# A recurrent-attention and gated-mixing kernel on one core: Wk loaded in quarters, one K group, one wait and one sum moved

## The chip, the cores and the metric

The kernel runs on one core of a Trainium2 chip. The core has a matrix engine (TensorE, in the rows PE, its weight loads PEld), a vector engine (VectorE, DVE), an activation engine (ScalarE, ACT), a general engine (GpSimd, POOL) and an engine that issues the DMAs (SyncE, SP). They run at their own pace and wait for each other through semaphores; each engine takes its instructions in the order of the program. TensorE multiplies a stationary operand, brought in by a weight load, with a moving operand that streams past, and writes its result to PSUM, which has eight banks. The metric is the time of one execution in device microseconds; of several runs the median counts.

## The reference

Two blocks are computed one after the other over a sequence of 2048 rows of 512 values, in bf16. Block A is attention with a recurrent memory: the sequence is cut into 64 segments of 32 rows, and 8 memory rows stand in front of each. What a segment's memory rows become is the memory of the next segment, so the 64 segments can't be computed side by side.

```
mem = mem0
for s in range(64):
    h = concatenate([mem, x_normed[32 * s : 32 * s + 32]])      # 40 rows
    q, k, v = h @ Wq, h @ Wk, h @ Wv                            # 32 heads of 128
    p = softmax(where(mask, q @ k.T * scale, -1e9))             # memory rows visible to all, the rest causal
    o = (p @ v) @ Wo
    mem, out[s] = o[:8], o[8:]
h = x + out
z = gelu(layernorm(h) @ w_in)                                   # block B, 512 -> 1792
z1, z2 = z[:, :896], layernorm(z[:, 896:])
h2 = h + (z1 * (w_sp @ z2 + b_sp)) @ w_out                      # w_sp mixes the 2048 rows
```

## The kernel before

All instructions are written out by a Python program that adds operations to the five engines' queues in one order (`em.add`, with the tokens each operation reads and writes); from the tokens it works out which waits each operation needs, and leaves out those that an earlier wait of the same engine covers already.

**Start.** x blocks and the weights are loaded by SP, in one queue. The last 8 of each segment's 32 x rows are treated apart: their Q, K and V are computed for 16 segments at once, ahead of the steps, as wide matmuls, in groups of 16 (four heads by four contraction chunks of 128, function `qkx_mm`, line 432). At the start 28 such groups run for the first chunks of segments: sixteen with Wq, then twelve with Wk (`start_x`). They rotate over four PSUM banks (`ebank`), and their evacuation alternates between ACT and DVE (`qkx_evac`, lines 441 and 443). Between them DVE computes the layer-norms of three x blocks (`ln_stats`, `ln_apply`, lines 379 to 389), with two small POOL operations in each. Then come the first wide V groups (line 457).

**The 64 steps.** A step has 32 stationary columns (8 memory rows, 24 x rows) in a slot of `hT`, in four contraction chunks `dc`. Chunk by chunk they are loaded as weights into the four column tiles of TensorE, 32 columns each, and four matmuls, one a tile, stream four different parts of the projection's weights past them. Four such matmuls of 512 columns are a "group" below. Where two groups in a row use the same chunk, the second can do without its weight loads: it is "held" (`tile_mm(..., held=True)`, recorded at line 515; with loads, line 514). A step is, in the order of TensorE:

- `QK(s, 0, 0)` and `QK(s, 0, 1)`: Q and K of the first 16 heads, chunk 0 first; then `mem_out(s - 1, 1)` (line 716), which transposes half of the former step's memory rows by matmuls with a selecting matrix; ACT copies them into `hT` (line 721), chunks 2 and 3. Then the other chunks.
- `QK(s, 1, 0)`: Q of the second 16 heads; `K1(s, 0, ...)` and `K1(s, 1, ...)`: K of the second 16 heads in two banks (3 and 7) of 256 columns, in the chunk order 3, 0, 1, 2 and 3, 0, 2, 1. ACT copies each out of PSUM (lines 551, 541), DVE transposes it (lines 563, 548).
- `S_half` (lines 585 and 591): scores of a half of the heads, with a mask that DVE puts into the bank ahead (line 575); exponential on ACT (line 599), sums over the keys on TensorE (line 606 and a held part), logarithm and reciprocal on ACT, normalisation on POOL and DVE (line 625, 631). Between them stand the groups of `V_half`.
- `PV_half` (lines 659 and 665): probabilities by V; line 665 uses the V of the 8 other rows (`Vx`, brought in by a DMA that step s - 1 issues). Then `Wo` (again line 514, with `cT`), `part_evac` and `mem_out(s, 0)`.
- In gaps, further work: wide groups for later segments, `WoX_mm` (line 743) for the 8 other rows, `F_group` (line 728), which sums four segments' results into a block of 128 rows, and from step 44 on the first matmuls of block B (`z2_narrow`, line 811).

Bank 7 serves, one after the other, the last K quarter-bank, PV and the second half of `Wo` (`OB2`), which DVE copies out (`part_evac`, line 709); `mem_out(s, 1)` reads that copy.

**Instruction blocks.** A planner (`plan`, `weight_of`, `block_cost`) counts TensorE's instructions from the program's first one, takes it that they are fetched in blocks of 256, and wants no block to begin at certain places of a step. It does so by `spare`: that many of a step's held groups are given their weight loads after all, which lengthens the step by four instructions each. `WAITS` and `STEP` stand for wait instructions of TensorE that the program can't count while it is written: so many before the loop, so many in each step. Looking four steps ahead, it takes the cheapest k from 0 to 8:

```
FETCH, FETCH0, WAITS, STEP = 256, 191, 11, 2
...
    return 4 if 338 <= place < 378 else 1 if 318 <= place < 338 or 148 <= place < 196 else 0
...
    n = 588 + 24 * (s % 4 == 2) + 8 * (s >= 3 * CK)
...
spare[0] = plan(s, pe_count[0] + WAITS + STEP * s)[1] if s else 0
```

**Behind the steps.** Block B's z2 for the last row blocks: row block 13 (`direct`) is computed straight from `z2_mm` in its narrow form (line 811), then the last `F_group(RB - 1, XB)`, the last `WoX_mm`, and the wide matmuls of z1, of the mixing (line 1352) and of the output (line 1476). `XB` is bank 3; the addition before this F (`h_done`, `F_add`, line 733, on DVE) reads it.

## Time and profile before

| | us |
|---|---|
| median of 3 runs | 843.62 (843.14 to 846.21) |
| the profiled execution | 844.33 |
| its span, first to last instruction | 842.6 |
| TensorE (PE) busy | 831.7, 99% |
| weight loads (PEld) busy | 435.8, 52% |
| VectorE (DVE) busy | 525.5, 62% |
| ScalarE (ACT) busy | 469.4, 56% |
| GpSimd (POOL) busy | 128.0, 15% |
| granted clock of TensorE | 0.999 |

The profile is of one execution; its times count from the span's start. A row of a timeline gives the start, the time, the engine, the line, the operation, what it writes and reads, and how many instructions are merged; in brackets stands the idle time before and what ended it. "128*32 128x512" is a matmul with 128 rows and 32 columns of weights and 512 columns of moving data. The end of a matmul is modelled, and four of a group run side by side, so starts are to be compared with starts. A row of the waits gives total time, number and longest wait. "Issue" is a wait that no semaphore explains.

### The profile page before, as it was taken

The numbers are of one execution on the slowest core, as the hardware profiler recorded it, in microseconds if no ns is written. First come the engines' busy times: TensorE is split into PE (matmuls) and PEld (weight loads), VectorE is DVE, ScalarE is ACT, GpSimd is POOL, SyncE is SP. The second block draws the span as 40 slices with busy tenths as digits, with TensorE's granted clock in tenths as the row PEclk, the third lists the DMA queues.
The fourth block names the chain that finished last, engine by engine and source line by source line (L and its number), as shares of the span: only waits on it lengthen the run. The fifth ranks groups of instructions, "written<-read, shape, count | busy, mean of one in ns | idle before, by whom it ended". The sixth has DMA issues, their size and how long they took to land.

```text
span 842.6 us, 45239 instructions
## 1 busy us (share of the span) xinstructions
PE 831.7 (99%) x22069; PEld 435.8 (52%) x19133; DVE 525.5 (62%) x1321; ACT 469.4 (56%) x1250; POOL 128.0 (15%) x340
## 2 busy tenths in 40 slices
PE   9999999999999999999999999999999999999998
PEld 9754555455555554545554555554555554444443
DVE  3556667676666666676666666766666666654443
ACT  3456665667676766667666666666666666500000
POOL 5011111111111111111111121111111113300000
PEclk9999999999999999999999999999999999999999
DMA  9962222322222232121223233233333479033001
GB/s 319 395 203 54 72 66 60 79 54 61 60 57 48 54 48 66 43 68 48 73 50 88 54 77 75 77 83 84 83 77 74 91 244 340 1 113 111 28 14 39
DMA packets 111877, 78.62 MB, mean 93 GB/s; under 512 B 65976, under 2 KB 103872, under 8 KB 111680
## 3 DMA queue, kind: packets, MB, share of 16 engines
q1 hardware_dynamic: 111680, 75.67, 32.2%
q8 instruction: 163, 2.67, 1.4%
q14 instruction: 34, 0.28, 0.1%
HBM read 43.16 MB, written 22.12 MB: 77 GB/s over the span
## 4 chain that ended last, share of the span: by engine, by line
PE 95%; DMA 2%; SPq 1%; DVE 1%; ACT 0%; issue 0%; POOL 0%
PE f_ps L514 45%; PE f_ps L515 12%; PE f_ps L1352 11%; PE f_ps L743 4%; PE f_ps L1476 3%; PE f_ps L659 3%; PE f_ps L1345 2%; PE f_ps L811 2%; PE f_ps L451 2%; PE f_ps L432 2%; DMA f_arena<-in_A_Wk_dram 2%; PE f_ps L585 1%; PE f_ps L606 1%; PE f_ps L457 1%; PE f_ps L716 1%; PE f_ps L665 1%
## 5 line engine op out<-in xcount | busy, mean ns | idle before, releaser
L514 PE MATMUL f_ps<-f_arena,f_hT 128*32 128x512 bf16 (+1 forms) x4996 | 358.3, 356 | 0.5 <-issue 0.3
L514 PEld LDWEIGHTS f_ps<-f_arena,f_hT 128*32 128x32 bf16 x4996 | 123.6, 96 | 152.4 <-issue 57.2
L515 PE MATMUL f_ps<-f_arena,f_hT 128*32 128x512 bf16 (+1 forms) x2172 | 173.4, 333 | 0.0
L551 ACT ACTIVATE f_Tst<-f_ps 128x512 bf16<-128x512 f32 x224 | 127.1, 597 | 60.7 <-PE f_ps L514 60.7
L514 PE MATMUL f_ps<-f_arena,f_cT 128*32 128x256 bf16 x3844 | 128.7, 272 | 1.2 <-ACT f_cT L678 0.5
L514 PEld LDWEIGHTS f_ps<-f_arena,f_cT 128*32 128x32 bf16 x3844 | 94.1, 96 | 29.4 <-ACT f_cT L678 19.6
L1352 PE MATMUL f_ps<-f_arena 128*128 128x512 bf16 x448 | 101.0, 379 | 0.6 <-DVE f_arena L1338 0.4
L563 DVE STREAM_TRANSPOSE f_QT<-f_Tst 128x256 uint32<-128x256 uint32 x128 | 57.1, 446 | 67.2 <-ACT f_Tst L551 67.2
L651 DVE CAST f_V_sb<-f_ps 128x512 bf16<-128x512 f32 (+1 forms) x128 | 71.0, 555 | 42.2 <-PE f_ps L514 42.2
L680 DVE TENSOR_SCALAR f_cT<-f_ps 128x320 bf16<-128x320 f32 x128 | 56.9, 487 | 28.5 <-PE f_ps L665 28.5
L1352 PEld LDWEIGHTS f_ps<-f_arena 128*128 128x128 bf16 x448 | 43.5, 98 | 54.0 <-DVE f_arena L1338 2.0
L709 DVE CAST f_part<-f_ps 128x256 bf16<-128x256 f32 x64 | 27.2, 425 | 63.5 <-PE f_ps L514 63.5
L599 ACT ACTIVATE f_E_sb<-f_ps 128x224 bf16<-128x224 f32 x128 | 46.2, 361 | 36.7 <-PE f_ps L591 36.7
L570 POOL COPY f_QT<-f_arena 128x128 uint32<-128x128 uint32 x64 | 18.8, 294 | 300.3 <-PE f_ps L591 300.1
L678 ACT ACTIVATE f_cT<-f_ps 128x320 bf16<-128x320 f32 x128 | 49.0, 435 | 23.0 <-PE f_ps L665 22.9
L721 ACT ACTIVATE f_hT<-f_ps 128x16 bf16<-128x16 f32 x126 | 23.3, 185 | 54.4 <-PE f_ps L716 54.0
L1358 DVE TENSOR_TENSOR f_arena<-f_ps,f_arena 128x512 f32<-128x512 f32 x28 | 19.3, 690 | 51.4 <-PE f_ps L1352 48.7
L575 DVE CAST f_ps<-f_mask 128x224 f32<-128x224 bf16 x128 | 47.0, 368 | 0.0
L621 ACT ACTIVATE f_R_sb<-f_R_sb 128x160 f32<-128x160 f32 x128 | 43.2, 338 | 4.0
L541 ACT ACTIVATE f_Tst<-f_ps 128x256 bf16<-128x256 f32 x128 | 42.2, 381 | 3.7
L700 POOL COPY f_cTx<-f_cT 128x256 bf16<-128x256 bf16 x64 | 25.4, 397 | 121.7 <-DVE f_cT L680 121.7
L707 ACT ACTIVATE f_part<-f_ps 128x256 bf16<-128x256 f32 x64 | 24.6, 385 | 31.8 <-PE f_ps L514 31.8
(130 smaller groups left out, 1216.1 us busy)
## 6 DMA issues: line engine op xcount, KB each, us to landing
wT_d<-f_wst SPq DMA_DIRECT2D x64, 128.0 KB, 3.1
f_arena<-wT_d SPq DMA_DIRECT2D x32, 256.0 KB, 4.7
f_arena<-in_A_Wk_dram SPq DMA_DIRECT2D x2, 2048.0 KB, 13.8
f_arena<-in_A_Wv_dram SPq DMA_DIRECT2D x2, 2048.0 KB, 23.3
f_arena<-in_A_Wo_dram SPq DMA_DIRECT2D x8, 512.0 KB, 9.3
f_Vx<-vext_d SPq DMA_DIRECT2D x63, 64.0 KB, 2.7
f_arena<-in_A_Wq_dram SPq DMA_DIRECT2D x3, 1024.0 KB, 10.5
vext_d<-f_Vs SPq DMA_DIRECT2D x24, 128.0 KB, 2.2
```

What stands on the lines that cost most here:

```text
L514: return e.matmul(out, lhsT=lhsT, rhs=rhs, start=start, stop=stop, skip_group_check=True, tile_position=(0, 32 * c))
L515: return e.add_instruction(mybir.InstMatmult(name=nc.get_next_instruction_name(), ins=[e.lower_ap(rhs), e.lower_ap(lhsT)], outs=[e.lower_a ...
L541: act(lambda e: e.activation(out=Tst[:, 1, 256 * k:256 * k + 256].rearrange("p (gi r) -> p gi r", r=2), in_=ps[:, bank, 0:256].rearrange(" ...
L551: act(lambda e: e.activation(out=Tst[:, tb, :].rearrange("p (C gi r) -> p C gi r", C=2, r=2), in_=ps[:, bank, :].rearrange("p (C r gi) -> ...
L563: dve(lambda e: e.transpose(out=dst, in_=Tst[:, mi, :].bitcast(U32)), reads=[("T", mi, 0), ("T", mi, 1)], writes=wr)
L575: dve(lambda e: e.tensor_copy(out=ps[:, bank, 0:224], in_=mask[:, :]), reads=["mask"], writes=[PB(bank)])
L599: act(lambda e: e.activation(out=E_sb[:, b, :], in_=ps[:, bank, 0:224], func=ACT.Exp, scale=scale, bias=SHIFT), reads=[PB(bank)], writes=[ ...
L621: act(lambda e: e.activation(out=R_sb[:, b, :], in_=R_sb[:, b, :], func=ACT.Exp, scale=-1.0, bias=RBIAS), reads=[("R", b)], writes=[("R", b)])
L651: dve(lambda e: e.tensor_copy(out=V_sb[:, b, cs], in_=ps[:, bank, cs]), reads=[PB(bank)], writes=wr)
L678: act(lambda e: e.activation(out=dst, in_=src, func=ACT.Copy, scale=UNSC), reads=[PB(PVB[c])], writes=[("cT", c)])
L680: dve(lambda e: e.tensor_scalar(out=dst, in0=src, scalar1=UNSC, scalar2=None, op0=ALU.mult), reads=[PB(PVB[c])], writes=[("cT", c)])
L1352: pe(lambda e: e.matmul(ps[:, bank, 0:TB], lhsT=z2[:, sc, fb * 128:(fb + 1) * 128], rhs=wTb[tb % 2][:, :, sc, :], start=(n == 0), stop=(n ...
```

## The change

Five edits:

1. Wk is loaded as quarter 0, quarter 1 and the second half, in place of two halves: one DMA more on SP's queue.
2. In steps from 1 on, `K1(s, 1, 0)`, the chunk-0 group of the last K quarter-bank (bank 7), runs directly behind `mem_out(s - 1, 1)`, with weight loads of its own, and opens the accumulation; it was the fourth of the K1 groups and held. `K1(s, 1, 3)` no longer opens it.
3. The last group of `V_half(s, 1)` waits, in its fourth column tile, for the DMA of the Vx rows, which line 665 waited for before.
4. Behind the steps, `F_group(RB - 1, XB)` comes after both z2 matmul sets of the direct row block, in place of between them.
5. The planner counts 592 for 588 instructions a step, 13 for 11 waits before the loop and 1 for 2 in each step.

```diff
-    def V_half(s, b, dcs=range(DC), held=None):
+    def V_half(s, b, dcs=range(DC), held=None, also=()):
...
-                   reads=[("hTx", (s // 4) % 3), ("hTm", s, dc // 2), ("W", 2, 2 * b), ("W", 2, 2 * b + 1)], writes=[PB(bank)])
+                   reads=[("hTx", (s // 4) % 3), ("hTm", s, dc // 2), ("W", 2, 2 * b), ("W", 2, 2 * b + 1), *(also if c == 3 else ())], writes=[PB(bank)])
...
-    for hf in range(2):
-        load_wh(1, hf)
+    load_w(1, 0)
+    load_w(1, 1)
+    load_wh(1, 1)
...
-    FETCH, FETCH0, WAITS, STEP = 256, 191, 11, 2
+    FETCH, FETCH0, WAITS, STEP = 256, 191, 13, 1
...
-        n = 588 + 24 * (s % 4 == 2) + 8 * (s >= 3 * CK)
+        n = 592 + 24 * (s % 4 == 2) + 8 * (s >= 3 * CK)
...
             mem_out(s - 1, 1)
+        if s:
+            K1(s, 1, 0, True, False, False)
         QK(s, 0, 1, (1,), 0, 2)
...
-        K1(s, 1, 3, True, False, bool(hold(True)))
+        K1(s, 1, 3, not s, False, bool(hold(True)))
         K1(s, 0, 0, False, False, False)
-        K1(s, 1, 0, False, False, bool(hold(True)))
+        if not s:
+            K1(s, 1, 0, False, False, bool(hold(True)))
...
-            V_half(s, 1, (2,))
+            V_half(s, 1, (2,), also=[("Vx", s % NVX)])
...
         z2_mm(rb, 0, zbank(), True)
+        z2_mm(rb, 1, zbank(), True)
         if k == 0:
             F_group(RB - 1, XB)
-        z2_mm(rb, 1, zbank(), True)
```

## The prediction

> **What bounds the kernel now.** I read the page first, then the waits of PE and PEld, then the timelines of the start, of two steps and of the seam behind the last step.
>
> ```profile
> span 842.6 us, 45239 instructions
> ...
> PE 831.7 (99%) x22069; PEld 435.8 (52%) x19133; DVE 525.5 (62%) x1321; ACT 469.4 (56%) x1250; POOL 128.0 (15%) x340
> ...
> GB/s 319 395 203 54 72 66 60 79 54 61 60 57 48 54 48 66 43 68 48 73 50 88 54 77 75 77 83 84 83 77 74 91 244 340 1 113 111 28 14 39
> ...
> q8 instruction: 163, 2.67, 1.4%
> ```
>
> ```profile
> PE f_ps L432 <- DMA f_arena<-in_A_Wk_dram: 1.4, 1, 1.4
> ...
> PEld f_ps L514 <- ACT f_hT L721: 33.6, 107, 0.4
> ```
>
> TensorE is the bound: 99% busy, and no other engine passes 62%. PE itself shows only one wait of over a microsecond that the change touches, 1.4 us for Wk. So no part can win much, and the prediction is a sum of small holes. "Busy" hides some of them: the end of a matmul is modelled, so a hole shows as a late start of the next group of four matmuls (one per column tile). I read starts against starts. The holes are of three kinds: the Wk wait; short waits at fixed places of each of the 64 steps; and irregular holes at the edges of instruction blocks (q8: 163 packets, 2.67 MB, so fetches of 16 KB, for 41,202 PE and PEld instructions, about one per 256).
>
> **Part 1, Wk in quarters and a half.** The first Wk group of matmuls needs only the first quarter of Wk.
>
> ```profile
> 21.93 0.41 PE L397 MATMUL f_ps<-f_ident,f_part 128*32 128x128 bf16 x16
> 23.77 2.84 PE L432 MATMUL f_ps<-f_hTe,f_arena 128*128 128x128 bf16 x48 [1.43 <-DMA f_arena<-in_A_Wk_dram]
> ...
> 39.39 1.90 PE L457 MATMUL f_ps<-f_arena,f_hTe 128*128 128x512 bf16 x8
> ...
> 23.74 0.69 DVE L443 CAST f_arena<-f_ps 128x512 bf16<-128x512 f32 x1
> ...
> 9.84 2.54 SPq L318 DMA_DIRECT2D f_arena<-in_A_Wk_dram  x2
> 12.42 7.58 SPq L318 DMA_DIRECT2D f_arena<-in_A_Wv_dram  x2
> ...
> f_arena<-in_A_Wk_dram SPq DMA_DIRECT2D x2, 2048.0 KB, 13.8
> f_arena<-in_A_Wv_dram SPq DMA_DIRECT2D x2, 2048.0 KB, 23.3
> ```
>
> The half issued at 9.84 lands at 23.64. Its second megabyte takes about 2.65 us at the page's 395 GB/s, so the first quarter lands near 21.0 and is there when PE is ready at 22.34 (21.93 + 0.41). The second, near 23.7, is wanted by the third group, later than 24. The 1.43 us wait on the DMA goes. But something else is late next. The groups of this stage rotate over four PSUM banks, and the second Wk group takes the bank of the fourteenth Wq group, whose evacuation is the DVE cast of 23.74. It ends at 24.43, held up behind the layer-norm of three x blocks, which does not depend on Wk. Today that second group starts at 23.77 + 0.9 = 24.67 (a third of the 2.84 us, less its part of the tail of the last matmul). It can't start before 24.49, 0.06 after the cast (the distance from an end on DVE or ACT to the start on PE in the rows of parts 2 and 3). **Gain 0.18 us, not 1.43**; PE will wait some 1.2 us for DVE in place of the DMA. Ends: 0, and 1.43 if that cast were earlier too. SP issues one DMA more, and the Wv loads queue behind it. They are issued from 12.42 on, take 23.3 us, and their first reader starts at 39.39: slack of over 3 us hides an issue of at most 2.5 us. One more wait stands in PE's stream, before the loop, inside the stretch that waits anyway: nothing.
>
> **Part 2, the quarter of the last K moved into the mem rows' shadow.** In each step from 1 on, the second half of mem_out transposes mem rows 2 and 3 by matmul, ACT copies them (L721), and the weights of contraction chunk 2 wait for the copy.
>
> ```profile
> 256.51 0.18 ACT L721 ACTIVATE f_hT<-f_ps 128x16 bf16<-128x16 f32 x1
> ...
> 256.30 0.39 PE L514 MATMUL f_ps<-f_arena,f_hT 128*32 128x512 bf16 x4
> 256.51 0.39 PE L515 MATMUL f_ps<-f_arena,f_hT 128*32 128x512 bf16 x4
> 256.75 0.61 PE L514 MATMUL f_ps<-f_arena,f_hT 128*32 128x512 bf16 x8
> 257.19 0.39 PE L515 MATMUL f_ps<-f_arena,f_hT 128*32 128x512 bf16 x4
> ...
> 257.83 0.82 PE L514 MATMUL f_ps<-f_arena,f_hT 128*32 128x512 bf16 x12
> 258.48 0.39 PE L515 MATMUL f_ps<-f_arena,f_hT 128*32 128x256 bf16 x8
> 258.70 0.28 PE L514 MATMUL f_ps<-f_arena,f_hT 128*32 128x256 bf16 x4
> 258.81 0.28 PE L515 MATMUL f_ps<-f_arena,f_hT 128*32 128x256 bf16 x4
> ...
> 648.36 0.39 PE L515 MATMUL f_ps<-f_arena,f_hT 128*32 128x512 bf16 x4
> ...
> 649.03 0.39 PE L515 MATMUL f_ps<-f_arena,f_hT 128*32 128x512 bf16 x4
> ```
>
> Three groups of 512 columns take 0.65 us undisturbed (257.83 to 258.48). Across the wait they take 0.68 (256.51 to 257.19) in step 21 and 0.67 (648.36 to 649.03) in step 60; over steps 2 to 62 the mean excess is 0.028 us. The copy ends at 256.69, PE goes on at 256.75. A group of 256 columns (0.11 us, 258.70 to 258.81) put before 256.30 moves the reader from 256.73, where two groups of 0.215 would let it start, to 256.84, past the copy: the hole closes. The group itself costs nothing net, being only moved. **Gain 63 x 0.028 = 1.76 us.** Its bank, number 7, was freed by the same part copy that mem_out waits for anyway, so no wait is added.
>
> It needs its own weight loads, four a step, where it used the loaded ones before. A pair of such held groups takes 0.22 (258.48 to 258.70), a loaded one 0.11: no difference, so I take zero, hidden beside the 0.11 us of matmul.
>
> What else the move does: the Q and first K projections end 0.11 us closer to the scores that need them.
>
> ```profile
> 259.34 0.45 DVE L563 STREAM_TRANSPOSE f_QT<-f_Tst 128x256 uint32<-128x256 uint32 x1
> 259.78 0.59 DVE L548 STREAM_TRANSPOSE f_KT<-f_Tst 128x128 uint32<-128x128 uint32 x2
> ...
> 259.36 0.66 ACT L541 ACTIVATE f_Tst<-f_ps 128x256 bf16<-128x256 f32 x2
> ...
> 260.45 0.27 PE L585 MATMUL f_ps<-f_QT,f_KT 128*32 128x40 bf16 x16
> ```
>
> DVE's transposes are a queue: Q's (259.34) shifts by 0.11 and ends at 259.90. The two of the last K start now at 259.78, released by ACT, whose two copies end at about 259.75 and 260.02; the first moves to some 259.83, the second, released at 260.02, needs to move by 0.00 to 0.05. They end at 260.37 now, and the second scores start at 260.45, a slack of 0.03 over the 0.06 from DVE's end to PE. So 0 to 0.02 us a step come back. I take 0; 63 x 0.02 = 1.3 us is the unfavourable end.
>
> **Part 3, the V rows' wait.** The wait for the Vx rows' DMA leaves PV, where it stands as an instruction of its own beside a wait for DVE, for the fourth column tile of a long V group. The DMA is issued a whole step ahead of its reader, so the wait holds up nobody for data.
>
> ```profile
> 262.34 0.33 DVE L625 TENSOR_TENSOR f_E_sb<-f_R_sb,f_E_sb 128x160 bf16<-128x160 f32 x1
> ...
> 262.66 0.21 PE L665 MATMUL f_ps<-f_E_sb,f_Vx 32*128 32x64 bf16 x4
> ...
> 262.73 0.31 PE L659 MATMUL f_ps<-f_E_sb,f_V_sb 32*128 32x40 bf16 x16
> ```
>
> Here the second PV half starts at 262.73, 0.06 after DVE's normalisation ends (262.67), and the Vx matmuls ahead of it have time to spare: an earlier 262.66 is lost there. That is so in 32 steps (12 to 43). In some 30 others PE runs through, and the pause ahead of L665 exceeds its neighbours' by 0.012 us. **Gain 30 x 0.012 = 0.35 us**; ends 0.75 (all steps) and a loss of 0.6 (0.01 in the V group in each).
>
> **Part 4, the F sums behind the second matmul of the direct row block.**
>
> ```profile
> 687.73 0.68 DVE L733 TENSOR_TENSOR f_hbuf<-f_ps,f_hbuf 128x512 bf16<-128x512 f32 x1
> ...
> 687.38 0.93 PE L811 MATMUL f_ps<-f_arena 128*32 128x448 bf16 x16
> 688.47 0.75 PE L728 MATMUL f_ps<-f_part,f_F_sb 128*32 128x512 bf16 x4 [0.16 <-DVE f_hbuf L733]
> ```
>
> Four groups of 448 columns (0.19 each, in proportion to 0.216) end at 688.14; F waits for its bank until DVE's addition ends at 688.41. The next four z2 groups fill 0.76 us of PE, past that end: **gain 0.33 us** (0 if the fetch hole that also falls on this F group, part 5, stays there). F's only reader, the WoX scatter into the same bank, stands well behind in the program, so F is late for nobody; the z2 result and its gelu come earlier.
>
> **Part 5, instruction blocks.** The stream grows by three instructions a step, so all block edges move, and the planner (new constants) spends other "unheld" loads. At some edges PE stands:
>
> ```profile
> 295.10 0.56 PE L514 MATMUL f_ps<-f_arena,f_cT 128*32 128x256 bf16 x8
> ...
> 475.22 0.28 PE L514 MATMUL f_ps<-f_arena,f_cT 128*32 128x256 bf16 x3
> 475.88 0.38 PE L514 MATMUL f_ps<-f_arena,f_cT 128*32 128x256 bf16 x5 [0.39 <-issue]
> ```
>
> Within one group 0.66 us pass from 475.22 to 475.88; the group of 295.10 lasts 0.56 where two quiet ones take 0.39. Between these 256-instruction edges from 295.10 to the last at 688.47 (L728 in the fence before: 0.75 where 0.39 is due) I count 13 such holes of over 0.08 us, 4.2 us together. They mostly follow blocks that begin shortly before PV, with many short instructions, which PE runs through fastest, so that the next fetch is late. Stepping the planner's formula through the steps of before, with 4 - 1 instructions more in each, I get 14 such blocks from step 24 on where there are 13 now. So I take no change, with 1.7 us to either side. The Trainium skill (Runtime: NRT & Kernel Launch, Instruction fetch mechanics) says that fetch goes in 16 KiB blocks of 256 instructions and that crossing one is mostly hidden. The block size agrees with the 2.67 MB in 163 fetches; 13 of some 160 edges not being hidden is what costs here.
>
> **The sum.** 0.18 + 1.76 + 0.35 + 0.33 = 2.6 us. The profiled execution takes 844.33 us (span 842.6, 1.7 around it); it would become 841.7. It stands 0.7 above the median of 843.62, within the runs shown. Against the median: **841.0 us**. A change of 0.5% (4.2 us) is about what a measurement of this kernel can tell; by that mark I forecast no change.
>
> **Rivals.**
> - The DVE queue takes the place of the mem rows (slower). If the full 0.11 us reaches the second K transpose, the second scores wait 0.11 - 0.03 = 0.08 us a step: 5.1 us lost, 1.76 won; with the other parts 843.62 + 2.5 = 846.1. It decides from a delay of 0.07 us on. For it: DVE's rows touch end to end. Against: the two K transposes wait for ACT today, which absorbs most.
> - The four loads a step don't hide (slower).
>
> ```profile
> L514 PEld LDWEIGHTS f_ps<-f_arena,f_cT 128*32 128x32 bf16 x3844 | 94.1, 96 | 29.4 <-ACT f_cT L678 19.6 <-issue 1.2
> ```
>
> A load costs the load path 94.1 / 3844 = 0.0245 us; 252 of them in the open are 6.2 us: 841.0 + 6.2 = 847.2. It decides from 0.010 us a load. Against it speaks the 0.11 of the group with loads at 258.70, as long as the held ones. The Trainium skill (TensorE: Matmul & The Clock Gate, Part 3, The mechanism) says that weight loads overlap matmuls in flight only where the row group differs; the four column tiles of a group here share theirs. By this rule the rival would hold; the rows at 258.48 and 258.70 don't agree with it for column tiles.
>
> - Block edges fall worse or better: 14 blocks at the 0.3 us that a hole costs on average, in place of 13 holes, is no change; all 14 at 0.5 us gives 7.0 for 4.2 us, 843.8, half of the holes gone 838.9. The dice are thrown anew.
> - The start wins the whole 1.43 us: 839.7. It needs DVE's cast at 23.74 to be earlier; its x blocks are loaded ahead of Wk as before, so I see no reason.
> - Part 2 does nothing, a later wait takes it: 842.8.
>
> **How the numbers follow.** The forecast, with block edges within 1 us of before, has 0.55. Block edges worse by more than that (about 843.5, at the worst 845): 0.13; better (839): 0.08. Part 2 does nothing: 0.09. The DVE queue: 0.06. The whole start: 0.06. The weight loads: 0.03. The forecast's own range is 839.4 to 842.6, from the ends of part 3 and 1 us of edges. Eight in ten are reached by taking in the better half of the edges' good side, the lost part 2 and the edges' bad side: **838.8 to 844.6**. Faster by over 0.5% means under 839.4: the better edges mostly, half of the whole start, a rest of the forecast's tail, 0.10. Slower by over 0.5% means over 847.8: a part of the weight loads and of the DVE queue together with bad edges, 0.04. The rest, 0.86, lies within 0.5%.
>
> **What the profile of after would show.** Part 1: no wait of L432 on the Wk DMA, but one of 1.2 us on the DVE cast L443 in the same place; the first Wv group earlier by 0.2 us, not by 1.4. Part 2: behind the mem rows' transposition a 256-column group, and three groups of 512 columns behind it in 0.65 us; the wait of PEld on ACT's L721 shorter by its half; the second scores still 1.09 us behind the first (260.45 against 259.36, where the held group of 258.48 and its followers end); the quiet steps 0.03 us shorter. Part 3: no change in the distance of the second PV half from DVE's L625 in steps 12 to 43. Part 4: L728 starts without a wait. Part 5: about a dozen holes at block edges, 3 to 6 us together, in other steps.
>
> Wrong would make it: a transposition chain on DVE that shifts by more than I read from its overlaps; a wait on bank 7 that I have missed, which would stand in front of the moved group in every step; or a planner whose count is off by a few instructions, so that block edges fall into PV in many steps.

## The result, and the profile after

The changed kernel takes 840.83 us (median of 6 runs, 840.04 to 840.97); beside it the kernel before took 845.41 (6 runs, 843.14 to 846.28). The ratio is 0.9951, with a 95% interval of 0.9936 to 0.9965. Repeated on another chip, it took 840.38 us beside 843.33, ratio 0.9969 (0.9957 to 0.9981). So the kernel is 1.6 to 5.4 us faster; 4.1 and 2.6 us are the middles of the two intervals. The forecast was 841.0 us, 2.6 less than the 843.62 that was known then.

The page of the changed kernel, profiled in an execution of 840.04 us:

```profile
span 838.3 us, 45576 instructions
...
PE 827.7 (99%) x22059; PEld 446.4 (53%) x19541; DVE 518.2 (62%) x1321; ACT 465.7 (56%) x1250; POOL 128.0 (15%) x340
```

TensorE is still the bound. The view of waits, as "engine line <- what it waited for: us in total, times, longest":

```profile
PE f_ps L432 <- DVE f_arena L443: 1.2, 1, 1.2
```

```profile
PEld f_ps L514 <- ACT f_hT L721: 30.7, 111, 0.4
```

The wait for Wk's DMA has become a wait for DVE of nearly the same length, and the weight loads wait for ACT's copies of the mem rows 2.9 us less (33.6 before). The timeline of the start (start, duration, engine and line; the idle time before it in brackets):

```profile
21.92 0.41 PE L397 MATMUL f_ps<-f_ident,f_part 128*32 128x128 bf16 x16
22.26 1.07 PE L432 MATMUL f_ps<-f_hTe,f_arena 128*128 128x128 bf16 x16
24.49 1.96 PE L432 MATMUL f_ps<-f_hTe,f_arena 128*128 128x128 bf16 x32 [1.16 <-DVE f_arena L443]
26.38 0.41 PE L397 MATMUL f_ps<-f_ident,f_part 128*32 128x128 bf16 x16
```

```profile
23.74 0.69 DVE L443 CAST f_arena<-f_ps 128x512 bf16<-128x512 f32 x1
```

The first Wk group runs at 22.26, as soon as PE is free. The second starts at 24.49, 0.06 after DVE's cast ends at 24.43. These last two times stand in the forecast to the hundredth; for the first it had 22.34.

Step 21 has these rows; they are about one microsecond earlier than the same step of before:

```profile
255.33 0.22 PE L716 MATMUL f_ps<-f_G_sb,f_part 128*32 128x8 bf16 x8
255.39 0.50 PE L514 MATMUL f_ps<-f_arena,f_hT 128*32 128x256 bf16 x8
255.72 0.39 PE L515 MATMUL f_ps<-f_arena,f_hT 128*32 128x512 bf16 x4
255.93 0.61 PE L514 MATMUL f_ps<-f_arena,f_hT 128*32 128x512 bf16 x8
256.36 0.39 PE L515 MATMUL f_ps<-f_arena,f_hT 128*32 128x512 bf16 x4
...
258.42 0.27 PE L585 MATMUL f_ps<-f_QT,f_KT 128*32 128x40 bf16 x16
...
259.51 0.27 PE L585 MATMUL f_ps<-f_QT,f_KT 128*32 128x40 bf16 x16
```

Behind the mem rows' transposition stand the moved quarter (four matmuls of the row at 255.39, 0.11 us) and four groups of 512 columns (0.215 each): 0.97 us are due, and 255.39 to 256.36 is 0.97. The hole is closed. ACT's copy and the weight loads that wait for it are there as before:

```profile
255.60 0.18 ACT L721 ACTIVATE f_hT<-f_ps 128x16 bf16<-128x16 f32 x1
```

```profile
255.84 0.20 PEld L514 LDWEIGHTS f_ps<-f_arena,f_hT 128*32 128x32 bf16 x8 [0.34 <-ACT f_hT L721]
```

The loads still start 0.06 us behind the copy, which ends at 255.78, but their matmuls are due only at 255.93. So the wait of the loads stays in the view of waits, and PE no longer sees it. The second scores still stand 1.09 us behind the first. At the seam:

```profile
684.02 0.68 DVE L733 TENSOR_TENSOR f_hbuf<-f_ps,f_hbuf 128x512 bf16<-128x512 f32 x1
```

```profile
683.67 1.69 PE L811 MATMUL f_ps<-f_arena 128*32 128x448 bf16 x32
685.18 0.39 PE L728 MATMUL f_ps<-f_part,f_F_sb 128*32 128x512 bf16 x4
685.39 1.90 PE L743 MATMUL f_ps<-f_arena,f_cTx 128*32 128x512 bf16 x32
```

The eight z2 groups run through, and F finds its bank free for 0.48 us (684.70 to 685.18).

Where the 4.3 us between the two profiled spans came from: the first scores start 0.32 us earlier (41.22 to 40.90); 62 steps, in the median 9.950 us long, became 9.919, 1.9 us; the seam gave 0.35. The rest, some 1.7 us, is the holes at block edges: 12 of over 0.1 us with 4.09 us together before, 8 with 2.36 after. That last item is what most of the experiments went to.

### The profile page after: what moved, and what is told of

The parts are those of the page before. It is cut to its first block, busy times and chain, and to the rows that moved or that the text cites. A ratio compares the mean times of both kernels' runs of the same rounds, so it can differ in the third digit from the quotient of the medians.

```text
span 838.3 us, 45576 instructions
## 1 busy us (share of the span) xinstructions
PE 827.7 (99%) x22059; PEld 446.4 (53%) x19541; DVE 518.2 (62%) x1321; ACT 465.7 (56%) x1250; POOL 128.0 (15%) x340
## 4 chain that ended last, share of the span: by engine, by line
PE 95%; DMA 1%; DVE 1%; ACT 1%; SPq 0%; issue 0%; POOL 0%
PE f_ps L514 47%; PE f_ps L1356 11%; PE f_ps L515 11%; PE f_ps L743 4%; PE f_ps L659 3%; PE f_ps L1480 3%; PE f_ps L1349 2%; PE f_ps L811 2%; PE f_ps L451 2%; PE f_ps L432 2%; DMA f_part<-in_A_x_dram 1%; PE f_ps L585 1%; PE f_ps L606 1%; PE f_ps L716 1%; PE f_ps L457 1%; PE f_ps L665 1%
## 5 line engine op out<-in xcount | busy, mean ns | idle before, releaser
L514 PE MATMUL f_ps<-f_arena,f_hT 128*32 128x512 bf16 (+1 forms) x5404 | 359.3, 351 | 0.3
L514 PEld LDWEIGHTS f_ps<-f_arena,f_hT 128*32 128x32 bf16 x5404 | 135.4, 96 | 138.7 <-issue 50.2
L551 ACT ACTIVATE f_Tst<-f_ps 128x512 bf16<-128x512 f32 x224 | 127.1, 597 | 65.3 <-PE f_ps L514 65.3
L515 PE MATMUL f_ps<-f_arena,f_hT 128*32 128x512 bf16 (+1 forms) x1764 | 146.7, 341 | 0.0
L721 ACT ACTIVATE f_hT<-f_ps 128x16 bf16<-128x16 f32 x126 | 23.2, 184 | 53.9 <-PE f_ps L716 53.4
L541 ACT ACTIVATE f_Tst<-f_ps 128x256 bf16<-128x256 f32 x128 | 42.1, 381 | 0.1
```

Source lines behind the costliest of these rows:

```text
L514: return e.matmul(out, lhsT=lhsT, rhs=rhs, start=start, stop=stop, skip_group_check=True, tile_position=(0, 32 * c))
L515: return e.add_instruction(mybir.InstMatmult(name=nc.get_next_instruction_name(), ins=[e.lower_ap(rhs), e.lower_ap(lhsT)], outs=[e.lower_a ...
L541: act(lambda e: e.activation(out=Tst[:, 1, 256 * k:256 * k + 256].rearrange("p (gi r) -> p gi r", r=2), in_=ps[:, bank, 0:256].rearrange(" ...
L551: act(lambda e: e.activation(out=Tst[:, tb, :].rearrange("p (C gi r) -> p C gi r", C=2, r=2), in_=ps[:, bank, :].rearrange("p (C r gi) -> ...
```

## The experiments

**1. Is it DVE's order that limits part 1?** The layer-norm work of three x blocks is spread over later evacuations, so that the cast the second Wk group waits for comes earlier. The second kernel does the same with Wk in two halves, as before. (Where an edit changes the number of instructions or waits, the planner's constants follow; these lines are left out here and below.)

```diff
-        if 11 <= n < 14:
-            ln_apply(n - 7)
-        if 10 <= n < 13:
-            ln_stats(n - 6)
+        if n in (11, 13, 15):
+            ln_apply(4 + (n - 11) // 2)
+        if n in (10, 11, 13):
+            ln_stats((4, 5, None, 6)[n - 10])
```

> The changed kernel, with DVE's evacuation of the fourteenth Wq group put ahead of the layer-norm work of the second and third x block (the same operations in another order). My theory: the quarters of Wk came in time, and only that cast holds the start. Then the wait of L432 on DVE (1.16 us) goes, the matmuls behind the second x transposition start near 25.3 instead of 26.72, the first scores come 1.3 to 1.4 us earlier, and the median falls from 840.8 to about 839.5. Rival: the second quarter, POOL's layer-norm operations or another bank hold PE next; then the start wins under 0.4 us and the median stays within 0.4 of the changed kernel's.

```diff
-    load_w(1, 0)
-    load_w(1, 1)
-    load_wh(1, 1)
+    for hf in range(2):
+        load_wh(1, hf)
```

> As e1_reorder, with Wk in two halves as before the change (and one wait fewer counted by the planner). My theory: both are needed. PE waits 1.4 us for Wk's DMA again, the first Wk matmul starts at 23.77, and the start is 1.2 to 1.4 us later than in e1_reorder; the median about 841. Rival: the order on DVE was all that mattered; then the start is as early as in e1_reorder.

Measured: with quarters and the new order 838.70 us beside 842.25, ratio 0.9965 (0.9951 to 0.9978); with halves and the new order 840.44, ratio 0.9977 (0.9967 to 0.9986). The timelines of the start, first with quarters, then with halves:

```profile
22.69 0.41 PE L397 MATMUL f_ps<-f_ident,f_part 128*32 128x128 bf16 x16
23.03 2.85 PE L432 MATMUL f_ps<-f_hTe,f_arena 128*128 128x128 bf16 x48
25.81 0.41 PE L397 MATMUL f_ps<-f_ident,f_part 128*32 128x128 bf16 x16
```

```profile
23.95 2.84 PE L432 MATMUL f_ps<-f_hTe,f_arena 128*128 128x128 bf16 x48 [1.39 <-DMA f_arena<-in_A_Wk_dram]
26.72 0.41 PE L397 MATMUL f_ps<-f_ident,f_part 128*32 128x128 bf16 x16
```

With quarters the three groups run through, though they begin 0.77 us later than in the changed kernel, because PE waited 0.7 us for Wq in this execution, and they end 0.57 earlier (25.81 for 26.38). With halves the 1.4 us wait for Wk's DMA is back. So the DMA and the DVE cast each hold the start by over a microsecond, one hidden behind the other, and taking away either alone gives almost nothing. The gain at the first scores is smaller than the 1.3 to 1.4 us that was expected, about 0.5, with that wait for Wq in it. The first scores start at 40.33 us with the new order (40.18 in experiment 6); without it, at 40.77 to 40.90 in six executions with the changed kernel's start, and at 41.17 and 41.59 in two others in which PE waited 0.4 and 0.7 us for Wq.

**2. Is it the moved quarter that shortens the steps, and how much does DVE absorb?** One kernel is the change without part 2; the other moves a second quarter as well.

```diff
-        if s:
-            K1(s, 1, 0, True, False, False)
...
-        if not s:
-            K1(s, 1, 0, False, False, bool(hold(True)))
+        K1(s, 1, 0, False, False, bool(hold(True)))
```

> The changed kernel without its part 2: the K group is back behind its neighbours and held, and the planner counts 588 again. My theory: the hole behind the mem rows comes back, three groups of 512 columns over it take 0.675 us for 0.646, the quiet step goes from 9.916 to 9.945 us, and without the block edges' share the time rises by 1.8 us (842.6; edges move it by up to 1.5 either way). Rival: the shorter step of the changed kernel comes from the V rows' wait; then the step stays at 9.92.

```diff
         if s:
             K1(s, 1, 0, True, False, False)
+            K1(s, 1, 1, False, False, False)
...
-        K1(s, 1, 2, False, False, bool(hold(True)))
-        K1(s, 1, 1, False, True, False)
+        K1(s, 1, 2, False, bool(s), bool(hold(True)))
+        if not s:
+            K1(s, 1, 1, False, True, False)
```

> The changed kernel with a second group of the same K quarter-bank (chunk 1) moved behind the mem rows as well. Q and the first K now end 0.22 us closer to the scores than before the change. My theory: DVE's transposes take up about 0.11 us and no more; the second scores wait some 0.08 us a step, the quiet step goes from 9.916 to about 10.0 us and the median to 845.5 or so. Rival: DVE's queue has room, as the first move cost nothing; the quiet step stays at 9.916 and the median within 1.5 us of 840.8.

Measured: without the move 841.53 us, ratio 0.9989 (0.9977 to 1.0001), and the quiet step is 9.947 us; with two quarters 845.18, ratio 1.0049 (1.0035 to 1.0063), quiet step 10.014. Step 21 without the move:

```profile
255.75 0.21 PE L716 MATMUL f_ps<-f_G_sb,f_part 128*32 128x8 bf16 x8
255.81 0.39 PE L514 MATMUL f_ps<-f_arena,f_hT 128*32 128x512 bf16 x4
256.02 0.39 PE L515 MATMUL f_ps<-f_arena,f_hT 128*32 128x512 bf16 x4
256.26 0.61 PE L514 MATMUL f_ps<-f_arena,f_hT 128*32 128x512 bf16 x8
```

The second of these groups lasts 0.24 where 0.215 is due: the hole of before is back, and the step with it. Part 2 is worth some 0.03 us a step (9.947 less the 9.915 to 9.919 of the changed kernel's two executions). With two quarters moved a new row stands in the waits of the weight loads, and its timeline shows it in a step:

```profile
PEld f_ps L585 <- DVE f_KT L563: 12.9, 54, 0.2
```

```profile
259.69 0.42 DVE L563 STREAM_TRANSPOSE f_KT<-f_Tst 128x256 uint32<-128x256 uint32 x1
...
259.70 0.60 ACT L551 ACTIVATE f_Tst<-f_ps 128x512 bf16<-128x512 f32 x1 [0.21 <-PE f_ps L514]
...
260.16 0.17 PEld L585 LDWEIGHTS f_ps<-f_QT,f_KT 128*32 128x32 bf16 x16 [0.24 <-DVE f_KT L563]
...
260.25 0.66 ACT L541 ACTIVATE f_Tst<-f_ps 128x256 bf16<-128x256 f32 x2
...
260.70 0.55 DVE L548 STREAM_TRANSPOSE f_KT<-f_Tst 128x128 uint32<-128x128 uint32 x2
...
261.33 0.27 PE L585 MATMUL f_ps<-f_QT,f_KT 128*32 128x40 bf16 x16
```

Now the first scores too wait for DVE's transposition (its end is 260.11), and the second stand 1.17 us behind them in place of 1.09. The step grows by 0.097. So the first quarter is taken in, and 0.097 of the second quarter's 0.11 is lost: the rival of the forecast is a true effect, and it decides between one quarter and two. Its engine is DVE only in part. The same rows of the changed kernel:

```profile
257.88 0.60 ACT L551 ACTIVATE f_Tst<-f_ps 128x512 bf16<-128x512 f32 x1 [0.21 <-PE f_ps L514]
...
258.43 0.66 ACT L541 ACTIVATE f_Tst<-f_ps 128x256 bf16<-128x256 f32 x2
```

The two copies of the last K (L541) run on ACT behind its copy of Q (L551). In the kernel before they start 0.057 us after that copy has ended, by the median of the steps 2 to 62. In the changed kernel and in this one they start 0.052 before its recorded end, so nothing is left between them: the first 0.11 us has used up all the room that ACT had. In this kernel they start 0.09 us behind the first scores, where they started 0.01 behind in the other two. The second of DVE's last transpositions (L548) starts 0.03 us behind ACT's second copy in all three kernels, so it is ACT's queue that it follows. By these rows some 0.08 us of the loss comes from ACT ahead of the second scores, and some 0.02 from DVE ahead of the first.

**3. Do the holes at block edges belong to the program?** First the changed kernel and the kernel before themselves, in a second execution each.

> The changed kernel itself, unaltered, next to the kernel before on this chip, as the yardstick for the three kernels run with it. If the steps of the prediction hold as the traces of before and after show them (start 0.3 us, 62 quiet steps of 0.031 us, F sums 0.3 us, and the holes at the block edges, 4.2 us before and 2.4 us after), it is 2.5 to 4.5 us faster than the kernel before, depending on how wide the holes are in the executions that are timed. Rival: the holes in one profiled execution are chance, and their mean over executions is the same in both kernels; then the difference is 2.4 us.

> The kernel before itself, unaltered, in a second profiled execution. Two executions of the changed kernel had their holes at block edges in different steps (32, 41, 42, 47, 48, 52 in one; 10, 13, 23, 24, 29, 32, 52 in the other), always at the same place modulo 256. New theory (the program fixes where a hole can be, and each execution throws anew which of the edges get one): here too the holes leave the steps 24, 27, 30, 36, 42, 45, 47, 51, 55 in about half of the cases, with a sum of 2.5 to 5 us in the steps, and the quiet step is 9.946 to 9.950 us. Rival (the holes belong to the program, and the 1.8 us between the profiled executions of before and after is the change's): the same steps with the same widths to 0.1 us, sum 4.0 to 4.4 us. The time is that of the kernel before, ratio 1.000 within 0.0015.

Measured: 840.38 us beside 843.33 (the ratio is given at the top), and 843.81 beside 843.63, ratio 0.9998 (0.9986 to 1.001). One place of the program in the first and second execution of the changed kernel, step 10:

```profile
154.89 0.35 PE L716 MATMUL f_ps<-f_G_sb,f_part 128*32 128x8 bf16 x8
```

```profile
154.82 0.21 PE L716 MATMUL f_ps<-f_G_sb,f_part 128*32 128x8 bf16 x6
155.57 0.18 PE L716 MATMUL f_ps<-f_G_sb,f_part 128*32 128x8 bf16 x2 [0.54 <-issue]
```

and another, step 42, in the same order:

```profile
473.31 0.27 PE L514 MATMUL f_ps<-f_arena,f_cT 128*32 128x256 bf16 x2
473.93 0.40 PE L514 MATMUL f_ps<-f_arena,f_cT 128*32 128x256 bf16 x6 [0.35 <-issue]
```

```profile
474.85 0.39 PE L514 MATMUL f_ps<-f_arena,f_cT 128*32 128x256 bf16 x8
```

A hole of 0.13 us is 0.71 in the other execution, and one of 0.61 is not there at all. All holes of over 0.1 us of the four executions, as step and width in us, measured as the late start of the next matmul against the usual distance at that place (the last one of before falls on the F group, F):

```
before, 1st  4.09: 24 .16  27 .22  30 .30  36 .36  42 .66  45 .49  47 .33  51 .31  52 .18  55 .41  55 .32  F .36
before, 2nd  5.42: 10 .40  15 .53  21 .37  24 .64  27 .48  33 .27  36 .44  37 .18  39 .21  42 .56  45 .19  51 .24  52 .45  60 .22  F .24
after, 1st   2.36: 10 .13  32 .30  41 .39  42 .61  47 .30  48 .21  52 .30  55 .12
after, 2nd   2.84: 10 .71  13 .28  23 .41  24 .43  29 .45  32 .29  52 .27
```

Three of the changed kernel's eight come back in its second execution, eight of the twelve of before, with other widths. The new theory holds in this: a program makes some edges likelier, and each execution throws anew how wide they get. The sum of 5.42 us is a little above the 2.5 to 5 that it expected. Without its holes an execution of before takes 844.33 - 4.09 = 840.24 and 845.41 - 5.42 = 839.99 us, one of the changed kernel 840.04 - 2.36 = 837.68 and 840.63 - 2.84 = 837.79: 2.4 us apart. This is what the change does in itself. By the same subtraction the timed medians would hold 2.1 to 5.3 us of holes for the kernel before (842.25 to 845.41 on the chips used), and 2.6 to 3.1 for the changed one. That is an estimate, which takes it that nothing but the holes differs between chips and executions.

**4. Do other block edges give another time?** Both kernels with 64 more instructions at the start of PE's stream, and the changed kernel with a planner that also avoids blocks which begin at the places 290 to 338 of a step.

```diff
-    spin(40)
+    for _ in range(72):
+        pe(lambda e: e.matmul(ps[:, 0, 0:64], lhsT=onesrc[:, 0:128], rhs=onesrc[:, 0:64], start=True, stop=True),
+           reads=["onesrc"], writes=[PB(0)])
```

> The changed kernel with 72 short warm-up matmuls of 64 columns in place of the 40 before the first transposes, so that every instruction behind them stands 64 places later in TensorE's stream and every block edge falls 64 instructions earlier in the work; nothing else differs, and the warm-up lies in time in which TensorE waits for data. Theory (block edges cost time): the holes move to other steps and their sum changes; the trace's holes account for the difference of the spans to within 0.5 us. The planner, which still reckons with the old edges, now has 9 blocks that begin at its places 338 to 378 where it had 6, so I expect 0.3 to 1.5 us more, 840.5 to 842.5 by the scale of the runs of after. Rival (the edges cost nothing, the irregular holes come from elsewhere): the holes stay in the same steps, and the time is that of the changed kernel within 0.3 us.

> The kernel before with the same shift of all block edges by 64 instructions. Theory (block edges cost time): the 13 holes of before leave their steps and others appear; with 10 blocks beginning at the places 338 to 378 where there were 4, but only 2 where there were 12 at 290 to 318, the sum may go either way, between 2.5 and 6 us where it was 4.2, and the time follows it: 840.5 to 844.5 on this chip, where before stands at 842.3. Rival (the edges cost nothing): holes in the same steps, time unchanged within 0.3 us.

```diff
-        return 4 if 338 <= place < 378 else 1 if 318 <= place < 338 or 148 <= place < 196 else 0
+        return 4 if 290 <= place < 378 else 1 if 148 <= place < 196 else 0
```

> The changed kernel with one number pair in the planner altered: a block that begins at the places 290 to 338 of a step is charged as much as one at 338 to 378 (4, where it was 0 below 318 and 1 above). Theory (the holes follow blocks that begin shortly before PV, 290 to 340 among them, as most of the 13 of before and 3 of the 8 of after do): fewer such blocks, holes of 1.0 to 2.0 us in place of 2.4, and a time 0.5 to 1.2 us below the changed kernel's. Rival (the holes follow the DMA traffic of the moment, and where a block begins doesn't matter): the sum of the holes stays at 2 to 3 us in other steps, and the time within 0.4 us of the changed kernel's. A part of the gain can be lost if the planner spends more loads and so makes more blocks.

Measured: 840.76 us for the changed kernel shifted (840.38 unshifted, on the same chip), 843.35 for the kernel before shifted (843.33 unshifted), and 839.44 with the wider window, ratio 0.9955 (0.9943 to 0.9967). The holes of the three profiled executions are 3.0, 2.8 and 4.3 us. My premise for the shifts was wrong: the planner counts from the real start of the stream, so it planned anew (the shifted changed kernel has 32 weight loads fewer in all, though the shift itself adds 32), and these two kernels are two more throws and not a planner put out of step. That neither time moves by more than 0.4 us says that two other plans did no worse; whether an edge costs by its place was not tested. The wider window left 4.3 us of holes in the execution that was profiled (841.64 us, the highest of its six), and its median is 0.9 us below the changed kernel's, which the intervals don't separate: whether it helps stays open.

What the holes do go with is the end of the instruction fetch. For all 14 profiled executions of this study (the two of before and after each, and ten variants) I took each edge between 42 and 683 us, the packet that the instruction queue fetched next, and the time at which PE came to the following edge:

```
end of the packet against PE's arrival   edges   with a hole over 0.1 us   mean hole, us
more than 1.4 us ahead                    1914      2                       0.006
1.4 to 1.2 ahead                           100     38                       0.07
1.2 to 1.0                                  59     51                       0.24
1.0 to 0.8                                  28     28                       0.45
0.8 to 0.6                                  12     12                       0.62
0.6 to 0.4                                   2      2                       0.65
```

The hole is what is missing of some 1.4 us between the packet's end and its first use: half of the holes fit 1.32 to 1.45 us. An edge's place is counted in the trace and known to a few instructions, so the 1.4 is uncertain by some 0.1 us. The packet takes as long in both cases (median 1.12 and 1.11 us), but it starts 1.30 us behind the edge before the 133 holes and 0.79 before the others, and a block with a hole behind it lasts 3.58 us where the others last 4.15. So by these traces a fast block together with a late start of the fetch makes a hole; no run moved a fetch on its own to test it. In step 10 of the changed kernel's two executions the packet ends 2.53 and 3.31 us behind its edge, and PE is at the next after some 3.9 and 4.0. What delays the start in one execution and not in the next stays open.

**5. Parts 3 and 4, and the weight loads.** One kernel has the V rows' wait and the F sums where they were before, the other gives every group that a planner's call would hold its own loads.

```diff
-            V_half(s, 1, (2,), also=[("Vx", s % NVX)])
+            V_half(s, 1, (2,))
...
-        z2_mm(rb, 1, zbank(), True)
         if k == 0:
             F_group(RB - 1, XB)
+        z2_mm(rb, 1, zbank(), True)
```

> The changed kernel with parts 3 and 4 undone: the V rows' wait stands ahead of PV again, and the F sums ahead of the second matmul of the direct row block. The two lie at different places of the trace. Part 3 by the prediction: 0.012 us in some 30 steps, the quiet step 9.915 to 9.927. By the reading of the trace of after (the 12 ns won ahead of L665 come back behind it, where PE waits for DVE in steps 12 to 43 and for ACT's copy L649 behind them): the pause ahead of L665 is 0.012 us longer in every step, and the quiet step is 9.915 within 0.002 us. Part 4: F waits for DVE's L733 again, and the seam from step 63 to the WoX scatter is 0.3 us longer. Time of both together 0.3 us above the changed kernel by the one reading, 0.7 by the other: not to be told apart by the clock, only in the steps.

```diff
     def hold(x):
+        return None
         if spare[0] > 0:
```

> The changed kernel with every held group given its own weight loads (some 1764 matmuls that use the weights already loaded get a load each, about 28 a step). Theory of the prediction (loads of these column-tile groups are hidden beside the matmuls): the quiet step stays at 9.915 us within 0.01, and the time is that of the changed kernel plus at most 0.5 us for some 7 more instruction blocks: 840.0 to 841.5. Rival (a load is in the open unless the row group differs, as the rule weighed in the prediction has it): at 0.0245 us a load 1764 of them are 43 us, 0.68 us a step, 883; already a quarter of it would show as 0.17 us a step.

Measured for the first: 841.96 us, ratio 0.9978 (0.9966 to 0.9989); quiet step 9.918. PV of step 51, in the changed kernel and then with the two parts undone:

```profile
561.10 0.27 PE L659 MATMUL f_ps<-f_E_sb,f_V_sb 32*128 32x40 bf16 x16
561.22 0.19 PE L665 MATMUL f_ps<-f_E_sb,f_Vx 32*128 32x64 bf16 x4
561.25 0.28 PE L659 MATMUL f_ps<-f_E_sb,f_V_sb 32*128 32x40 bf16 x16
561.37 0.21 PE L665 MATMUL f_ps<-f_E_sb,f_Vx 32*128 32x64 bf16 x4
561.50 0.61 PE L743 MATMUL f_ps<-f_arena,f_cTx 128*32 128x512 bf16 x7
```

```profile
561.20 0.28 PE L659 MATMUL f_ps<-f_E_sb,f_V_sb 32*128 32x40 bf16 x16
561.33 0.21 PE L665 MATMUL f_ps<-f_E_sb,f_Vx 32*128 32x64 bf16 x4
561.36 0.28 PE L659 MATMUL f_ps<-f_E_sb,f_V_sb 32*128 32x40 bf16 x16
561.46 0.21 PE L665 MATMUL f_ps<-f_E_sb,f_Vx 32*128 32x64 bf16 x4
561.60 0.62 PE L743 MATMUL f_ps<-f_arena,f_cTx 128*32 128x512 bf16 x8
```

Without the wait the first half of PV takes 0.12 in place of 0.13, and the second 0.12 in place of 0.10. Both take 0.40 us from end to end. ACT's copy of V in the changed kernel:

```profile
560.87 0.39 ACT L649 ACTIVATE f_V_sb<-f_ps 128x256 bf16<-128x256 f32 x1
```

It ends at 561.26, and the third group of the second half starts 0.055 us behind it, so the time won ahead is waited there. From the first PV matmul to the work behind PV both kernels take the same in the median of each stretch: 0.40 us in the steps 1 to 11, 0.47 in 12 to 43 and 0.40 in 44 to 62. Part 3 gives nothing in any of them. At the seam of this kernel:

```profile
685.36 0.40 PE L728 MATMUL f_ps<-f_part,f_F_sb 128*32 128x512 bf16 x4 [0.16 <-DVE f_hbuf L733]
```

F waits again, and from the WoX sums (L753) to the scatter (L743) it is 2.29 us for 1.94: part 4 gives 0.35. This kernel's median lies 1.6 us above the changed kernel's, which ran on another chip; 0.35 is accounted for, and the rest can be its holes: its profiled execution of 840.69 had 3.2 us of them and is the second lowest of its ten.

Measured for the second: 839.60 us, ratio 0.9955 (0.9940 to 0.9970), quiet step 9.918. Its page:

```profile
PE 829.2 (99%) x22069; PEld 481.1 (57%) x20801; DVE 518.0 (62%) x1321; ACT 465.3 (56%) x1250; POOL 127.4 (15%) x340
```

20801 - 19541 = 1260 loads more (504 matmuls of the 512-column form are still held), and neither the step nor the time is longer. At the forecast's rate, 0.0245 us a load, they would have cost 30.9 us in the open. The Trainium skill (TensorE: Matmul & The Clock Gate, Part 3, The mechanism) says in one sentence that a load overlaps the matmuls in flight only where the row group differs; for the column tiles of this kernel the runs don't agree. Another sentence of the same section also lets a load go ahead that targets the background weight buffer, which the forecast did not weigh; the runs agree with that one, but don't show that this is how it comes about.

**6. A version that might beat both.** The new DVE order of experiment 1 and the wider window of experiment 4 together.

> The changed kernel with DVE's layer-norm work of three x blocks spread over later copies (as in the first of these experiments) and with the planner's wider window. If the start's gain stands (first scores 0.6 to 1.3 us earlier than in the changed kernel) and the window brings nothing, because the holes are thrown anew in each execution: 838.5 to 839.5. If the wider window has a gain of its own (it stood 0.9 us below the changed kernel): 837.6 to 838.4.

Measured: 839.93 us, ratio 0.9959 (0.9945 to 0.9973). The start gains as before (first scores at 40.18 us, no wait of L432), the window shows nothing, and the time is 0.4 us above the range that was expected. Of the versions faster than the kernel before, the spread order, the wider window, both together and the loads for all have ratios of 0.9965, 0.9955, 0.9959 and 0.9955 on different chips, each with some 0.0013 to either side, so none of them can be put ahead of the changed kernel by the clock; by the trace the DVE order is 0.6 us better at the start.

## Why the prediction was right, and where not

**Part 1 was right in size and reason.** 0.18 us was forecast for the Wk groups; the row behind them starts at 26.38, and in the kernel before it stands at 26.54:

```profile
26.54 0.41 PE L397 MATMUL f_ps<-f_ident,f_part 128*32 128x128 bf16 x16
```

That is 0.16 us, and the wait on DVE has the place and the length that were named. Experiment 1 shows the rest of the wait to be DVE's order. Some 0.15 us more at the start is a block-edge hole near 29.8 us that is not in the changed kernel's trace.

**Part 2 was right.** 0.028 us a step was forecast, 0.031 was measured (0.028 to 0.032 when undone), 1.9 us for 1.76. That 0 to 0.02 would come back through DVE did not happen: the distance of the scores is 1.09 us as before. The rival's loss is there, but begins above one quarter, and most of it comes from ACT's copies, where the forecast had DVE's queue (experiment 2). The forecast was right that the K transpositions wait for ACT, which takes in the shift; it did not see that one quarter uses up ACT's room to the end. The slack of 0.03 us that it read ahead of the second scores is nearer 0.01: the last transposition ends 0.083 us ahead of them before, and 0.073 with two quarters, where PE waits for it. One sign was wrong: the weight loads' wait on L721 was to shrink by half and went from 33.6 to 30.7 us, because the loads still wait for the copy, only ahead of the time at which PE needs them.

**Part 3 was mis-sized: 0.35 us was taken, 0 was measured.** The step that failed is "in some 30 others PE runs through": the longer pause ahead of L665 was taken to be on the path, and what PE waits for behind it was left out. It is DVE in the steps 12 to 43, as the forecast said, and ACT's copy L649 in the later ones; for the steps 1 to 11 the runs show the zero, and what takes the time back there stays open.

**Part 4 was right**: 0.33 forecast, 0.35 measured when undone.

**Part 5 took no change, and this is the term that the comparison of the two profiled executions seems to contradict**: 4.09 us of holes went to 2.36. The repeats show that such a difference is within what one program does from execution to execution (4.09 and 5.42 before; 2.36 and 2.84 after; up to 4.3 in variants of the changed kernel). The argument that I gave, fourteen blocks beginning shortly before PV for thirteen, was no good reason for the zero: the steps with a hole change though the blocks don't. The part of it that stands is that the holes mostly follow blocks that PE runs through fast (3.58 us against 4.15); but the fetch starts late too, and that varies. Whether the changed kernel also has fewer holes in the mean is not settled: the timed medians say, by the estimate of experiment 3, between 0.6 (3.2 less 2.6) and 2.2 (5.3 less 3.1), and two traces of each don't decide it. The Trainium skill (Runtime: NRT & Kernel Launch, Instruction fetch mechanics) has the crossing of a block mostly hidden; here 133 of 2115 were not, and they cost 1.3 to 5.4 us an execution, as much as the whole change.

**The sum**: 2.6 us was forecast from the parts; without holes the executions are 2.4 apart, which is the forecast less part 3 and a little more from part 2. The difference between the medians, 4.6 in the first measurement and 2.95 in the second, has the holes of the day in it. So the forecast of 841.0 hit 840.83 with the right parts but one, and with luck: it was counted from a median of 843.62, while the kernel before took 845.41 beside the changed one. Counted from there, or from the 843.33 of the other chip, the same 2.6 us give 842.8 and 840.7 for 840.83 and 840.38. The first ratio, 0.9951, lies just inside the 0.5% that the forecast called no change, and its interval reaches beyond. The forecast's own range, 839.4 to 842.6, doesn't follow from the ends named for it, which added up give 839.6 to 842.95; the results lie in both.

The weight loads cost nothing, as taken. "The whole start" could be had, but with the work on DVE in another order, which the change did not touch.

## What to carry to other kernels

When a wait is taken away, look up what the same instruction would have waited for next: here a cast on DVE held the second group for 1.2 us once a 1.4 us wait for a DMA was gone, and only both together were worth removing. A pause that is seen on the bounding engine is a gain only if the work behind it isn't held by another engine at a fixed distance; measure from end to end of the stretch, not at the pause. And before holes at instruction-block edges are explained by a program's layout, profile the same program a second time.

## What the runs showed that I had not expected

- The holes of one and the same program move between executions: two of the changed kernel share three of eight and seven. The sum in one execution was 1.3 to 5.4 us over the 14 profiled ones.
- No fetched block was used much sooner than some 1.4 us after the end of its packet without a hole (131 of the 133 holes are at edges where the packet ended less than 1.4 us ahead, and of the 1914 edges with more only two have one).
- 1260 weight loads more, in groups that could have used the weights already loaded, cost no time that can be measured: 9.918 us a step with them, 9.915 to 9.919 without.
- The start of the first scores varies by 0.8 us between eight executions that share the changed kernel's order at the start (40.77 to 41.59 us); in the two latest PE waited for Wq, which none of the edits had moved.
